# Two of the four block sums of the feed-forward made in one piece, and a small key copy moved to GpSimd

## The chip, the cores and the metric

The kernel runs on one core of a Trainium2 chip. The metric is the device time of one execution in microseconds (us); lower is better. The core has five engines that run their own instruction queues side by side and wait for each other through semaphores: TensorE (PE in the profile, its weight loads PEld), VectorE (DVE), ScalarE (ACT), GpSimd (POOL) and SyncE (SP, which here issues most of the DMAs).

## What is computed

Attention with a few global key columns and a local window, and behind it a mixing layer with a low-rank part and a feed-forward part. Batch 4, 8 heads, 768 positions, head size 64, 8 global columns, a window of 96; model width 512, hidden width 2048, rank 32.

```python
scores = scale * np.matmul(q, k.transpose(0, 1, 3, 2))
is_global = pos[None, :] < int(n_global)
is_local = (rel >= 0) & (rel < int(n_local))
scores = scores - slopes[:, None, None] * dist      # by head
scores = np.where(is_global | is_local, scores, -1000000000.0)
a = np.exp(scores - max); a = a / (sum(a) + 1e-09)
x = np.matmul(a, v)                                 # (4, 768, 512)
u = x + (x.transpose(0, 2, 1) @ U @ V).transpose(0, 2, 1)
out = u + np.maximum(u @ w_ch1, 0.0) @ w_ch2
```

## The kernel before

**Attention.** Two heads of one batch make a pair, 128 partitions wide when transposed; there are 16 pairs, `i` from 0 to 15, four to a batch. For each pair q and k are loaded, cast to 16 bits and turned to `qT` and `kT` (head dimension on the partitions): by TensorE for pairs 0 to 7 (`st_T`), by transposing DMAs for pairs 8 to 15 (`turn`). Positions lie in six blocks of 128. A query block needs its own key block (`kT`) and the one before it, and the eight global columns. For the second kind there is a tile `kA`: the key blocks 0 to 4 with the first eight columns of each written over by the global columns. For pairs 8 on, `st_K` makes it with two instructions: ScalarE copies columns 8 to 127 of each block (L339), VectorE the eight global columns into all five blocks, 128x40 elements (L340).

The scores (L365 with `kT`, L372 with `kA`) come in three parts into the PSUM tile `sc`; VectorE adds the bias and writes `sp` (L403), ScalarE takes the exponential (`ep`, L415), TensorE multiplies by v (`ob`, L428 and L432), VectorE divides (L437, L451) into `x_sb`. GpSimd casts that to 16 bits (`x16`, L454) and casts the next v (L142).

**The low-rank part.** Per pair: `st_M1` multiplies `x16` by U (L463), ScalarE copies the small result (L467), `st_MT` transposes it on TensorE (L480) and VectorE copies it to `tmp16` (L481, `tmp` in the profile); `st_M3` multiplies by V into the PSUM tile `sc` (L517, with `tmp` as its moving operand), VectorE adds it to `x_sb` (L522), GpSimd casts the sum (L525), and a DMA transposes it to `uT` (`st_X`).

**The feed-forward part.** Positions are taken in groups of 256, three to a batch. An "up" unit is eight matmuls of 256 columns (L631) and a relu by ScalarE (L636) into `htr`; a group has eight ups. The groups of batch 0 are multiplied by the second weight directly (L666). For the nine groups of batches 1 to 3, called `WG`, the second product is done in seven block products instead of eight. `htr` is split into four blocks of 128 positions by 1024 hidden units: a11, a12 (first 128 positions), a21, a22 (last 128). Four sums of them are made on VectorE (L555):

- s1 = a21 + a22
- s2 = s1 - a11
- s3 = a11 - a21, written over a21
- s4 = a12 - s2

and four such sums `t1` to `t4` of the weight's blocks once. The products, each eight matmuls of 256 columns (L684), run in the order x1 (a11), y1 (a12), x2 (s2), y2 (s1), x3 (s3), y3 (s4), x4 (a22); the x accumulate in the bank `cx`, the y in `cy`, and after each VectorE adds the part to `x_sb` (L689). When a result is whole a DMA stores it.

**The order.** Everything is issued in one order written out by hand, so each engine's queue is what the loop over `i` issues. Between the steps of the attention, `fill` issues a given number of units: an up of a coming group or a product of the one before, mostly in turn. The relu's values come in two halves: the ups are issued so that after the fourth of a group the first half of the hidden units of each of a11, a12, a21 and a22 is there and after the eighth the rest (`mk_up`, `queue_sums(0)` and `queue_sums(1)`). Each half queues its four sums of 512 elements, in the order s1, s2, s4, s3, in the deque `jobs`, due two units later; after each unit one job that is due is issued (two if more than four are waiting). A product that needs sums issues what is still queued first, through `need`. The tiles s1, s2 and s4 have one buffer each. In the loop `st_MT` (L480, L481) and `st_M3` (L517) have one unit between them; `st_K` follows `st_MT` at once.

Of the kernel before, what the change touches and what calls it, by code (L numbers as in the profile page):

```python
# [16 lines left out]
ALU = mybir.AluOpType  # L17
# [3 lines left out]
def kernel(  # L21
# [13 lines left out]
    nc = tc.nc  # L35
# [30 lines left out]
    HJ = NJC // 2  # L66
# [20 lines left out]
    def ps_cps(name):  # L87
        return psum.tile([P, 512], FP32, name=name, tag="cps", bufs=2)
# [247 lines left out]
    def st_K(i):  # L336
        kT = kts[i]
        kA = kp.tile([P, NSB - 1, P], FP16, name="kA", tag="kA")
        nc.scalar.copy(kA[:, :, NG:], kT.rearrange("d (n p) -> d n p", n=NSB)[:, 0:NSB - 1, NG:])  # L339
        nc.vector.tensor_copy(  # L340
            kA[:, :, 0:NG], kT[:, 0:NG].unsqueeze(1).broadcast_to((P, NSB - 1, NG))
        )
        kas[i] = kA
# [208 lines left out]
    def queue_sum(name, part, out_, a, b_, op, wait=0):  # L552

        def go():
            nc.vector.tensor_tensor(out_, a, b_, op)  # L555
            have.add((name, part))
        (slow if name[0] == "t" else jobs).append((count[0] + wait, go))

    def need(*names):

        for queue, kind in ((jobs, tuple), (slow, str)):
            while not all(n in have for n in names if isinstance(n[0], kind)):
                queue.popleft()[1]()
# [19 lines left out]
    def weight(w, j):  # L583
        return tw[w][:, j] if w != "t3" else tw[w][j // 2][:, j % 2]
# [11 lines left out]
    def queue_group(b, g):  # L596
# [3 lines left out]
        cell = {}  # L600
# [3 lines left out]
        last = (b, g) == (B - 1, NFG - 1)  # L604

        def queue_sums(k):

            h = cell["htr"]
            if k == 0:
                for x in (1, 2, 4):  # L610
                    cell[f"s{x}"] = ffp.tile([P, HJ, P], FP16, name=f"s{x}", tag=f"s{x}", bufs=1)
                cell.update(a11=h[:, 0:HJ, 0:P], a12=h[:, HJ:NJC, 0:P],
                            a21=h[:, 0:HJ, P:FT], s3=h[:, 0:HJ, P:FT], a22=h[:, HJ:NJC, P:FT])
            js = slice(k * HJ // 2, (k + 1) * HJ // 2)
            for name, a, b_, op in (
                ("s1", "a21", "a22", ALU.add), ("s2", "s1", "a11", ALU.subtract),
                ("s4", "a12", "s2", ALU.subtract), ("s3", "a11", "a21", ALU.subtract),
            ):
                queue_sum((name, b, g), k, cell[name][:, js], cell[a][:, js], cell[b_][:, js], op, wait=0 if last else 2)

        def mk_up(at):
            jp = at // 2 + (at % 2) * NJC // 4 if split else at

            def go():
                if jp == 0:
                    cell["htr"] = ffp.tile([P, NJC, FT], FP16, name="htr", tag="htr", bufs=3)
                hps, done = begun.pop(jp) if jp in begun else (ps_th("hps"), 0)
                for k in range(2):
                    jt = 2 * jp + k
                    for dc in range(done, NDC):  # L630
                        nc.tensor.matmul(  # L631
                            hps[:, k * FT:(k + 1) * FT],
                            w1_16[:, dc, jt * P:(jt + 1) * P], uT[:, dc, ts],
                            start=(dc == 0 and k == 0), stop=(dc == NDC - 1 and k == 1),
                        )
                nc.scalar.activation(  # L636
                    cell["htr"][:, 2 * jp:2 * jp + 2].rearrange("p j t -> p (j t)"), hps, AF.Relu
                )
                if split and at % 4 == 3:
                    queue_sums(at // 4)  # L640
            return go

        def store(n, cs=slice(0, DM)):
            def go():
                nc.sync.dma_start(out[b, n * P:(n + 1) * P, cs], x_sb[:, n, cs])
            if b:
                go()
            else:
                kept.append(go)
# [25 lines left out]
        def mk_product(bank, half, a, w, dst, first=False, done=None):  # L675

            def go():
                if bank not in cell:
                    cell[bank] = ps_cps(bank)
                need(*(((a, b, g), k) for k in range(2) if a[0] == "s"))  # L680
                need(*((w, k) for k in range(4 if w == "t3" else 2) if w[0] == "t"))
                ps = cell[bank][:, half]
                for j in range(HJ):
                    nc.tensor.matmul(  # L684
                        ps, cell[a][:, j], weight(w, j), start=(first and j == 0),
                        stop=(done is not None and j == HJ - 1), skip_group_check=True,
                    )
                n, cs = dst
                nc.vector.tensor_tensor(x_sb[:, n, cs], ps, x_sb[:, n, cs], ALU.add)  # L689
                for what in done or ():  # L690
                    store(*what)
            return go
# [111 lines left out]
    for i in range(NP, NPAIR + 2):  # L804
        b, hp = divmod(i, NP)
# [73 lines left out]
        if NPE <= i + 1 < NPAIR:  # L879
            st_K(i + 1)  # L880
# [52 lines left out]
```

## Time and profile before

| What | Value |
| --- | --- |
| Runs shown: median (lowest to highest), 3 runs | 231.4 us (230.68 to 231.84) |
| The profiled execution's own time | 231.74 us |
| Its span, first to last instruction | 230.0 us |
| Granted TensorE clock, mean over the span | 1.00 |
| Relu, L636, ScalarE | 96 instructions, 56.4 us busy |
| Sums of the relu's values, L555, VectorE | 72 instructions of 512 elements, 33.4 us busy |
| Global key columns, L340, VectorE | 8 instructions, 1.3 us busy |
| `tmp`, L481, VectorE | 12 instructions, 3.4 us busy |

A line of a timeline has the start and the duration in microseconds, the engine, the line of the kernel, the operation, what it writes and reads, the shape and the count of merged instructions; in brackets how long its engine stood idle before it and what ended that. VectorE's instructions overlap a little at their ends. A line of a source view has the smallest, the median and the largest duration in ns and the first and last start. Busy shares are means over the whole span: the attention runs up to about 175 us, the direct products to about 90 us, the seven-product groups from about 99 us to the end.

### The profile page before, as it was taken

What the parts mean: (1) busy time and instruction counts of PE and PEld (TensorE: products, weight loads), DVE (VectorE), ACT (ScalarE), POOL (GpSimd) and SP (SyncE); (2) the same over time, 40 slices, a digit from 0 to 9 for tenths busy, and PEclk for the clock granted to TensorE, in tenths of its full rate; (3) what the DMA queues carried; (4) which work ended last, traced back from release to release, by engine and by line L of the source; (5) the groups of instructions that cost most, each with busy time, mean ns of one, the idle gap of its engine ahead of it and who ended that gap; (6) DMA issues with size and microseconds to landing.
All of it is one profiled execution on the core that took longest, in us unless ns stands there. A gap on an engine that the chain in (4) does not pass through costs nothing.

```text
span 230.0 us, 5877 instructions
## 1 busy us (share of the span) xinstructions
PE 220.7 (96%) x2418; PEld 171.1 (74%) x2420; DVE 161.5 (70%) x337; ACT 125.8 (55%) x196; POOL 72.3 (31%) x115
## 2 busy tenths in 40 slices
PE   7989899999999999999999999999999999999993
PEld 2456568788745445888888878888988888888882
DVE  3799876749577979597989897989764444444452
ACT  6787747786805253968485847292732433333320
POOL 6499708297553323123313131313111000000000
PEclk9999999999999999999999999999999999999999
DMA  6999996979999879897979994951321202010022
GB/s 185 335 283 281 281 291 90 321 135 180 191 163 206 201 180 228 203 239 175 261 202 219 242 200 102 144 158 25 88 69 36 94 0 94 0 67 27 10 84 93
DMA packets 86563, 36.68 MB, mean 160 GB/s; under 512 B 74152, under 2 KB 83592, under 8 KB 86536
## 3 DMA queue, kind: packets, MB, share of 16 engines
q1 hardware_dynamic: 81480, 32.01, 57.5%
q0 software_dynamic: 5056, 4.29, 12.4%
q8 instruction: 19, 0.31, 0.6%
q14 instruction: 8, 0.07, 0.1%
HBM read 27.46 MB, written 6.29 MB: 147 GB/s over the span
## 4 chain that ended last, share of the span: by engine, by line
PE 67%; DVE 15%; DMA 7%; ACT 4%; POOL 2%; issue 1%; SPq 0%; ACTq 0%
PE hps L631 25%; PE cx L684 13%; PE cy L684 10%; PE cps L666 8%; DMA w<-in_moe_w_ch_dram 6%; DVE sp L403 3%; PE sc L365 2%; ACT ep L415 2%; DVE x_sb L451 2%; PE tp L254 2%; PE ob L432 2%; DMA kst<-in_k_dram 2%; PE sc L517 1%; PE ob L428 1%; DVE s L555 1%
## 5 line engine op out<-in xcount | busy, mean ns | idle before, releaser
L631 PE MATMUL hps<-uT,w 128*128 128x256 f16 x756 | 96.0, 273 | 0.0
L636 ACT ACTIVATE htr<-hps 128x512 f16<-128x512 f32 x96 | 56.4, 598 | 58.0 <-PE hps L631 57.9
L631 PEld LDWEIGHTS <-w 128*128 128x128 f16 x756 | 70.5, 98 | 9.9 <-issue 0.2
L403 DVE SCALAR_TENSOR_TENSOR sp<-sc,relcat 128x1024 f32<-128x1024 f32 (+1 forms) x36 | 40.7, 1131 | 9.1 <-ACT ep L415 4.8
L415 ACT ACTIVATE ep<-sp 128x1408 f16<-128x1408 f32 x24 | 33.1, 1380 | 0.7 <-DVE sp L403 0.6
L684 PEld LDWEIGHTS <-htr 128*128 128x128 f16 x288 | 27.5, 98 | 3.6
L454 POOL CAST x<-x_sb 128x384 f16<-128x384 f32 x27 | 14.5, 538 | 49.8 <-DVE x_sb L451 45.7
L689 DVE TENSOR_TENSOR x_sb<-cx,x_sb 128x256 f32<-128x256 f32 x36 | 15.2, 422 | 18.3 <-PE cx L684 17.7
L666 PE MATMUL cps<-w,htr 128*128 128x512 f16 x96 | 24.0, 379 | 0.4 <-DMA w<-in_moe_w_ch_dram 0.4
L525 POOL CAST x<-x_sb 128x768 f16<-128x768 f32 x12 | 11.0, 916 | 40.8 <-DVE x_sb L522 40.8
L684 PEld LDWEIGHTS <-s 128*128 128x128 f16 x216 | 20.2, 98 | 2.9 <-DVE s L555 0.6
L689 DVE TENSOR_TENSOR x_sb<-cy,x_sb 128x256 f32<-128x256 f32 x27 | 11.4, 423 | 12.5 <-PE cy L684 12.3
L365 PEld LDWEIGHTS <-kT 64*128 64x128 f16 x192 | 8.3, 93 | 13.7 <-issue 12.4
L451 DVE TENSOR_TENSOR x_sb<-ob,rcp 128x384 f32<-128x384 f32 x30 | 16.7, 558 | 1.0
L365 PE MATMUL sc<-qT,kT 64*128 64x128 f16 x192 | 16.8, 221 | 0.3 <-DVE x_sb L522 0.2
L432 PE MATMUL ob<-v,ep 128*128 128x65 f16 x192 | 16.4, 193 | 0.0
L432 PEld LDWEIGHTS <-ep 128*128 128x128 f16 x192 | 13.8, 98 | 3.1 <-ACT x L787 0.7
L428 PE MATMUL ob<-vA,ep 128*128 128x65 f16 x160 | 14.5, 194 | 1.2 <-DVE vA L316 1.2
L142 POOL CAST v<-vst 128x768 f16<-128x768 f32 x16 | 14.0, 877 | 2.9 <-DMA vst<-in_v_dram 2.9
L372 PE MATMUL sc<-qT,kA 64*128 64x128 f16 x160 | 14.3, 217 | 0.6 <-DVE kA L290 0.4
L666 PEld LDWEIGHTS <-htr 128*128 128x128 f16 x96 | 8.4, 97 | 8.5 <-issue 0.5
L522 DVE TENSOR_TENSOR x_sb<-sc,x_sb 128x768 f32<-128x768 f32 x12 | 11.5, 956 | 4.6 <-PE sc L517 4.6
(109 smaller groups left out, 315.0 us busy)
## 6 DMA issues: line engine op xcount, KB each, us to landing
qst<-in_q_dram SPq DMA_DIRECT2D x16, 384.0 KB, 4.7
kst<-in_k_dram SPq DMA_DIRECT2D x16, 384.0 KB, 6.1
vst<-in_v_dram SPq DMA_DIRECT2D x16, 384.0 KB, 4.0
out_dram<-x_sb SPq DMA_DIRECT2D x23, 256.0 KB, 3.1
w<-in_moe_w_ch_dram POOLq DMA_DIRECT2D x8, 512.0 KB, 8.1
vA<-v SPq DMA_DIRECT2D x8, 152.3 KB, 3.0
out_dram<-x_sb SPq DMA_DIRECT2D x2, 128.0 KB
uT<-x SPq DMA_TRANSPOSE x12, 3.1
```

Of the source, the lines that this page charges most:

```text
L365: nc.tensor.matmul(scs[hi][:, o:o + P], kT[r, kb * P:(kb + 1) * P], qT[r, kb * P:(kb + 1) * P], start=(o == 0 and not on_pe), stop=(o + P ...
L403: nc.vector.scalar_tensor_tensor(out=sps[i][:, :, c0:c0 + tot], in0=both[:, :, 0:tot], scalar=qk_scale / slope[2 * (i % NP)], in1=relfs[c0 ...
L415: nc.scalar.activation(eps[i][:, hi], sps[i][:, hi], AF.Exp, scale=slope[2 * (i % NP)])
L428: nc.tensor.matmul(ob[:, qi], ep[:, OF[qi - 1]:OF[qi - 1] + P], vA[:, qi - 1, hi], start=True, stop=False,)
L432: nc.tensor.matmul(ob[:, qi], ep[:, DG[qi]:DG[qi] + P], vt[:, qi, hi], start=(qi == 0), stop=True,)
L451: nc.vector.tensor_tensor(xo, ob[:, :, 0:D], rb, ALU.mult)
L454: nc.gpsimd.tensor_copy(x16, xo)
L631: nc.tensor.matmul(hps[:, k * FT:(k + 1) * FT], w1_16[:, dc, jt * P:(jt + 1) * P], uT[:, dc, ts], start=(dc == 0 and k == 0), stop=(dc == ...
L636: nc.scalar.activation(cell["htr"][:, 2 * jp:2 * jp + 2].rearrange("p j t -> p (j t)"), hps, AF.Relu)
L666: nc.tensor.matmul(cps, htr[:, jc, t * P:(t + 1) * P], w2_16[:, jc], start=(b > 0 and jc == 0), stop=(jc == NJC - 1),)
L684: nc.tensor.matmul(ps, cell[a][:, j], weight(w, j), start=(first and j == 0), stop=(done is not None and j == HJ - 1), skip_group_check=True,)
L689: nc.vector.tensor_tensor(x_sb[:, n, cs], ps, x_sb[:, n, cs], ALU.add)
```

## The change

Two edits. The global key columns of pairs 8 to 15 are copied by GpSimd instead of VectorE. And for all groups of `WG` but the last, s3 and s4 are no longer made by halves: nothing is queued for them at the first half, and at the second one instruction of 1024 elements each, in the order s1, s2, s3, s4 (s1 and s2 by halves as before). The last group keeps its halves, with s3 ahead of s4. The products wait for one part of s3 and s4 instead of two.

```diff
@@ st_K @@
-        nc.vector.tensor_copy(
+        nc.gpsimd.tensor_copy(
             kA[:, :, 0:NG], kT[:, 0:NG].unsqueeze(1).broadcast_to((P, NSB - 1, NG))
         )
@@ queue_sums @@
-            js = slice(k * HJ // 2, (k + 1) * HJ // 2)
             for name, a, b_, op in (
                 ("s1", "a21", "a22", ALU.add), ("s2", "s1", "a11", ALU.subtract),
-                ("s4", "a12", "s2", ALU.subtract), ("s3", "a11", "a21", ALU.subtract),
+                ("s3", "a11", "a21", ALU.subtract), ("s4", "a12", "s2", ALU.subtract),
             ):
-                queue_sum((name, b, g), k, cell[name][:, js], cell[a][:, js], cell[b_][:, js], op, wait=0 if last else 2)
+                parts = {k: slice(k * HJ // 2, (k + 1) * HJ // 2)}
+                if name in ("s3", "s4") and not last:
+                    parts = {0: slice(0, HJ)} if k else {}
+                for part, js in parts.items():
+                    queue_sum(
+                        (name, b, g), part, cell[name][:, js], cell[a][:, js], cell[b_][:, js],
+                        op, wait=0 if last else 2,
+                    )
@@ mk_product @@
-                need(*(((a, b, g), k) for k in range(2) if a[0] == "s"))
+                need(*(((a, b, g), k) for k in range(2 if last or a in ("s1", "s2") else 1)
+                       if a[0] == "s"))
```

In VectorE's queue this takes out 24 instructions. Where before the second halves of a group stood as s1, s2, s4, s3 with the other work between them, they now stand as s1, s2, s3 (whole), s4 (whole); in three of the five groups whose sums lie within the attention, `L481` comes straight behind s4, as it came straight behind the second half of s3 before.

## The prediction

> **What bounds the kernel now.** I read the page's busy shares first, then TensorE's timeline for the places where it stands still, and last VectorE's and GpSimd's timelines around those places.
>
> ```profile
> PE 220.7 (96%) x2418; PEld 171.1 (74%) x2420; DVE 161.5 (70%) x337; ACT 125.8 (55%) x196; POOL 72.3 (31%) x115
> ...
> 104.56 1.04 PE L631 MATMUL hps<-uT,w 128*128 128x256 f16 x8
> 105.81 0.50 PE L517 MATMUL sc<-tmp,v16w 128*128 128x128 f16 x6 [0.21 <-DVE tmp L481]
> ...
> 136.57 0.61 PE L684 MATMUL cx<-t,s 128*128 128x256 f16 x4
> 137.46 0.61 PE L684 MATMUL cx<-t,s 128*128 128x256 f16 x4 [0.28 <-DVE s L555]
> ...
> 138.99 1.04 PE L684 MATMUL cy<-t,s 128*128 128x256 f16 x8
> 139.86 0.50 PE L517 MATMUL sc<-tmp,v16w 128*128 128x128 f16 x6
> ...
> 171.33 1.04 PE L631 MATMUL hps<-uT,w 128*128 128x256 f16 x8
> 172.48 0.49 PE L517 MATMUL sc<-tmp,v16w 128*128 128x128 f16 x6
> ```
>
> Columns: start, duration, engine, line, operation, count. TensorE bounds. Eight 256-column matmuls follow each other at 0.87 us a group (138.99 to 139.86), 0.109 each, so where TensorE stands still can be computed. After 104.56 the next was due at 105.43 and began at 105.81: 0.38 us lost, site A. Four from 136.57 were due to end their turn at 137.01, the fifth began at 137.46: 0.45 lost, site B0. At 139.86 (site B) L517 starts on time. After 171.33 it was due at 172.20 and came at 172.48: 0.28 lost, site C. I found no other wait of over 0.15 us for VectorE after 95 us; the remaining irregularities are fixed steps of about 0.1 us around the half-height score matmuls. So all that VectorE costs TensorE while the sums run is 0.38 + 0.45 + 0.28 = 1.11 us. After C TensorE waits for nothing up to the end, so a microsecond lost at any site is a microsecond at the end.
>
> VectorE just before A, B and C:
>
> ```profile
> 104.48 0.42 DVE L555 TENSOR_TENSOR s<-htr,s 128x512 f16<-128x512 f16 x1
> 104.81 0.42 DVE L689 TENSOR_TENSOR x_sb<-cx,x_sb 128x256 f32<-128x256 f32 x1
> 105.14 0.42 DVE L555 TENSOR_TENSOR htr<-htr 128x512 f16<-128x512 f16 x1
> 105.48 0.28 DVE L481 CAST tmp<-ob 128x128 f16<-128x128 f32 x1
> ...
> 138.20 0.41 DVE L689 TENSOR_TENSOR x_sb<-cx,x_sb 128x256 f32<-128x256 f32 x1
> 138.53 0.41 DVE L555 TENSOR_TENSOR s<-htr,s 128x512 f16<-128x512 f16 x1
> 138.86 0.41 DVE L555 TENSOR_TENSOR htr<-htr 128x512 f16<-128x512 f16 x1
> 139.20 0.28 DVE L481 CAST tmp<-ob 128x128 f16<-128x128 f32 x1
> ...
> 171.47 0.42 DVE L689 TENSOR_TENSOR x_sb<-cx,x_sb 128x256 f32<-128x256 f32 x1 [0.68 <-PE cx L684]
> 171.81 0.42 DVE L555 TENSOR_TENSOR htr<-htr 128x512 f16<-128x512 f16 x1
> 172.14 0.28 DVE L481 CAST tmp<-ob 128x128 f16<-128x128 f32 x1
> ```
>
> L481 makes `tmp`, which L517 loads; only one unit of the feed-forward (0.87 us) lies between TensorE's L480, which L481 waits for, and L517. What stands just ahead of L481 on VectorE is therefore critical, and at A, B and C that is a sum of this change. L517 starts 0.05 us after L481 ends (105.76 to 105.81). At B L481 ends at 139.48 and L517 is due at 139.86, so B has 0.38 - 0.05 = 0.33 us to spare. At C VectorE had stood idle 0.68 us for TensorE's `cx` and could not have begun sooner.
>
> **The change, part by part.** *Sums.* Eight of the nine groups have s3 and s4 made as one 1024-element instruction each instead of two of 512. The source view has the durations:
>
> ```profile
> L555 DVE TENSOR_TENSOR s<-htr x18: 415/416/935, 96.0 to 220.8; 128x512 f16<-128x512 f16 x18
> ...
> L555 DVE TENSOR_TENSOR t<-w,t x4: 682/682/1121, 72.6 to 89.1; 128x1024 f16<-128x1024 f16 x4
> ```
>
> (minimum, median, maximum in ns.) A half takes 0.416 us, and its successor starts 0.335 us after it (105.14 to 105.48, 0.08 overlapped). A whole is not there for these tiles; the weight sums of the same size take 0.682, so 0.60 from start to start. Per group 4 x 0.335 - 2 x 0.60 = 0.14 us of VectorE is saved, 1.1 us over eight. That alone is worth nothing: VectorE is not the bound. What counts is where the longer instructions fall. In the order of the changed kernel the second halves of s1 and s2 are followed by L403 (where a score tile is due), s3 whole, the `cx` addition, s4 whole, L481; before, one half stood on either side of `cx`, or two behind it.
>
> At C `cx` is released by TensorE, so all ahead of it is hidden in the 0.68 us of idling; behind it a whole replaces a half: L481 is later by 0.682 - 0.416 = 0.27 us, and L517 with it. At B `cx` follows L403 and is released before both sums; two wholes replace two halves, 0.53 us later, less 0.33 to spare: 0.20 us. At A the bounds are wider. `cx` (a group of eight begun at 103.64, its last result at 104.68) can be added at 104.72 at best; then s4 runs 105.05 to 105.73 and L481 starts at 105.65 instead of 105.48: +0.17. At worst L403 still starts at 103.61: s3 from 104.48, `cx` from 105.08, s4 from 105.41, L481 at 106.01: +0.53. The first halves of s3 and s4 (99.48 to 100.46) are gone from ahead of this, but the second half of s1 waits for ScalarE's relu (101.83 + 0.60 = 102.43) and starts at 102.45 instead of 102.61, so 0.16 of the gain survives: 0.53 - 0.16 = 0.37, and I take 0.35.
>
> The other pairs have no whole sum between L480 and L481 and start L517 on time with some 0.3 us to spare, as at B. The users of s3 and s4 are far off: at A s3 would be done by 105.16 at worst for the product at 108.32, s4 by 106.1 for the one at 110.83. In the late groups the second half of s2 starts at 196.94, so s3 would run from 197.3 to 198.0 and, behind the `cx` addition of 198.41, s4 from 198.75 to 199.4, for products that TensorE's timeline has at 200.76 and 202.51. The relu's buffer is held no longer than by these same products.
>
> *Key columns.* Eight copies of 128x40 (166 ns each) leave VectorE: at most 1.3 us, behind L481 and ahead of L522, which waits for TensorE's L517 anyway. On GpSimd the nearest row is its own 128x32 copy of the same kind (L295, 212 ns). They stand there behind the cast of v (L142) and ahead of the cast of x (L525), before which GpSimd idles 3.0 to 4.8 us in this stage; 0.21 us vanishes in that. If this cover went, x's transposing DMA would start 0.21 later each time. The copy comes sooner than before: behind the cast ending at 104.39 instead of at 105.68, for score matmuls (L372) at 108.06. Its only new wait there is for the DMA that lands kT (3.3 to 4.5 us after issue, 99.96 + 3.5 = 103.5). No DMA is added or moved on SP or GpSimd. L372 now waits for ScalarE and GpSimd, eight more wait instructions on TensorE's queue; queue waits of other engines show 17 to 21 ns. Bounds 0 and 8 x 0.021 = 0.17 us; the weight loads run ahead, so I take 0.
>
> *GpSimd against VectorE.*
>
> ```profile
> 95.87 0.83 POOL L525 CAST x<-x_sb 128x768 f16<-128x768 f32 x1 [3.99 <-DVE x_sb L522]
> 96.04 0.94 DVE L555 TENSOR_TENSOR s<-htr 128x512 f16<-128x512 f16 x1 [0.23 <-ACT htr L636]
> ```
>
> A sum that starts while GpSimd copies takes 0.94 instead of 0.42 us and ends 0.28 after the copy. B0 is that too: the second half of s2 took 0.94 from 136.47, against the cast of v (136.11 to 137.14). A new copy of 0.21 us can lengthen a sum by that. At B0 it would run from 137.14 and push s2, which TensorE waits for, by 0.21 if it is taken first; the sum was already waiting, so I take 0 and keep 0.21 for the range. The Trainium skill speaks against this part of the change: "SBUF — State Buffer", section "Who interferes with whom", has the port that VectorE's second SBUF input comes through shared with GpSimd, and whoever starts first keeps it for the whole instruction. The two rows above agree; what would follow here is the second rival.
>
> **Sum.** 0.35 (A) + 0.20 (B) + 0.27 (C) + 0 = 0.82 us. On the profiled execution, 231.74 us with a span of 230.0 and 1.74 around it, that is 232.56; it lies 0.34 above the median of the runs, 231.4, which so becomes **232.2 us**, 0.35% slower. Ends: 0.17 + 0 + 0.27 = 0.44 and 0.53 + 0.20 + 0.27 + 0.17 = 1.17: 231.8 to 232.6.
>
> **Rivals.** *VectorE's relief pays.* If the sums, thinned by 2.4 us, reached A, B0 and C in time, all 1.11 us would go: 230.3. For it: VectorE is 9.15 of 10 us busy from 130 to 140. Against: C's addition waited for TensorE, A's sums for ScalarE, B0's for GpSimd. 0.10.
>
> *GpSimd holds VectorE off at the wrong moment.* A at its worst, because GpSimd's cast of v moves ahead with the additions that it follows and meets the second half of s1 (+0.53), the new copy getting in first at B0 (+0.21), B 0.20, C 0.27: 1.21, so 232.6, and with one more sum held for a whole cast of v (0.5) ahead of L481 233.1. For it: eleven sums after 95 us are already lengthened. Against: most of these meet no wait of TensorE. It decides once a hold ends less than one sum ahead of L481. 0.25.
>
> *B0 goes.* With sums moved, the second half of s2 may miss the cast of v: -0.45 against +0.82, 231.8. Against: what precedes it there (additions, L451) is unchanged and still sets the cast off. 0.13.
>
> **Chances.** The forecast has 0.52. About 0.5% of the time, 1.16 us, is what a measurement tells from none. Faster than 230.24: half of the first rival and a little for the scatter of runs (230.68 to 231.84), 0.07. Slower than 232.56: two thirds of the second rival, 0.17, and the upper part of the forecast with that scatter, 0.20: 0.37. Within: 0.56. The range, 231.1 to 233.1, leaves out the first rival and the tails.
>
> **What would show it.** In the changed profile: six L555 instructions a group with two near 0.68 us; L517 late by 0.6 to 0.9 at A, some 0.2 at B, 0.55 at C; GpSimd's key copy near 0.21 us and done over 2 us before L372; L684 never waiting for s3 or s4. Wrong it would be if L517 came sooner than before at A or C, if L372 waited for GpSimd, or if TensorE lost time where these traces show none.

## The result and the profile after

| | Kernel before | Changed kernel |
| --- | --- | --- |
| Median of all runs | 231.39 us (22 runs) | 232.43 us (22 runs) |
| Ratio to before, 95% interval | | 1.0048 (1.0027 to 1.007) |
| Profiled execution: time, span | 231.74, 230.0 us | 232.32, 230.5 us |

The changed kernel is slower by about half a percent, 0.6 to 1.6 us by the interval. Ratios are over runs in the fast state; the trace of e2 below is of a run in the slow one (235.18 us), with a granted clock of 0.91 between 20 and 40 us and of 1.00 from 80 us on, where the places read lie.

TensorE's timeline after the change, at the same places as before (the ups are now line L637, the products L691, the additions L696):

```profile
104.31 1.04 PE L637 MATMUL hps<-uT,w 128*128 128x256 f16 x8
105.86 0.49 PE L517 MATMUL sc<-tmp,v16w 128*128 128x128 f16 x6 [0.51 <-DVE tmp L481]
...
136.61 0.61 PE L691 MATMUL cx<-t,s 128*128 128x256 f16 x4
137.50 0.61 PE L691 MATMUL cx<-t,s 128*128 128x256 f16 x4 [0.28 <-DVE s L555]
...
139.03 1.04 PE L691 MATMUL cy<-t,s 128*128 128x256 f16 x8
140.12 0.49 PE L517 MATMUL sc<-tmp,v16w 128*128 128x128 f16 x6
...
171.58 1.04 PE L637 MATMUL hps<-uT,w 128*128 128x256 f16 x8
173.00 0.50 PE L517 MATMUL sc<-tmp,v16w 128*128 128x128 f16 x6 [0.39 <-DVE tmp L481]
```

With 0.109 us a matmul, L517 was due at 105.18, 139.91 and 172.45. It came 0.68 late at A (0.38 before), 0.21 at B (0 before) and 0.55 at C (0.28 before). B0 lost 0.45, as before. At B no bracket stands, because the matmul before it ends, as modelled, at 140.07; only the start tells. The three growths are 0.30 + 0.21 + 0.27 = 0.78 us.

VectorE's timeline there:

```profile
103.99 0.68 DVE L555 TENSOR_TENSOR htr<-htr 128x1024 f16<-128x1024 f16 x1
104.59 0.41 DVE L696 TENSOR_TENSOR x_sb<-cx,x_sb 128x256 f32<-128x256 f32 x1
104.92 0.68 DVE L555 TENSOR_TENSOR s<-htr,s 128x1024 f16<-128x1024 f16 x1
105.52 0.28 DVE L481 CAST tmp<-ob 128x128 f16<-128x128 f32 x1
...
138.57 0.68 DVE L555 TENSOR_TENSOR htr<-htr 128x1024 f16<-128x1024 f16 x1
139.16 0.70 DVE L555 TENSOR_TENSOR s<-htr,s 128x1024 f16<-128x1024 f16 x1
139.78 0.28 DVE L481 CAST tmp<-ob 128x128 f16<-128x128 f32 x1
...
170.50 0.69 DVE L555 TENSOR_TENSOR htr<-htr 128x1024 f16<-128x1024 f16 x1
171.72 0.42 DVE L696 TENSOR_TENSOR x_sb<-cx,x_sb 128x256 f32<-128x256 f32 x1 [0.54 <-PE cx L691]
172.07 0.68 DVE L555 TENSOR_TENSOR s<-htr,s 128x1024 f16<-128x1024 f16 x1
172.66 0.28 DVE L481 CAST tmp<-ob 128x128 f16<-128x128 f32 x1
```

At C whole s3 lies in the time in which VectorE waited for `cx` anyway (idle 0.68 us there before, 0.54 now); whole s4 lies behind `cx` and ahead of L481. At B both lie ahead of L481 without idle time. The page has VectorE at 155.9 us busy instead of 161.5: less work, more time.

### The profile page after: what moved, and what is told of

Its sections match the earlier page's. It is cut to its first block, busy times and chain, and to the rows that moved or that the text cites. A ratio compares the mean times of both kernels' runs of the same rounds, so it can differ in the third digit from the quotient of the medians.

```text
span 230.5 us, 5876 instructions
## 1 busy us (share of the span) xinstructions
PE 220.7 (96%) x2418; PEld 170.9 (74%) x2420; DVE 155.9 (68%) x313; ACT 125.7 (55%) x196; POOL 72.9 (32%) x123
## 4 chain that ended last, share of the span: by engine, by line
PE 70%; DVE 11%; DMA 9%; POOL 3%; ACT 3%; issue 1%; SPq 1%
PE hps L637 27%; PE cx L691 13%; PE cy L691 10%; PE cps L672 8%; DMA w<-in_moe_w_ch_dram 6%; DMA vst<-in_v_dram 3%; PE sc L365 3%; DVE sp L403 3%; PE ob L432 2%; DVE s L555 2%; PE sc L517 2%; DVE x_sb L451 1%; PE ob L428 1%; PE tp L254 1%; PE sc L372 1%
## 5 line engine op out<-in xcount | busy, mean ns | idle before, releaser
L637 PE MATMUL hps<-uT,w 128*128 128x256 f16 x756 | 95.9, 273 | 0.0
L637 PEld LDWEIGHTS <-w 128*128 128x128 f16 x756 | 70.6, 98 | 9.7
L403 DVE SCALAR_TENSOR_TENSOR sp<-sc,relcat 128x1024 f32<-128x1024 f32 (+1 forms) x36 | 40.7, 1131 | 8.9 <-ACT ep L415 4.8
L691 PEld LDWEIGHTS <-htr 128*128 128x128 f16 x288 | 27.5, 98 | 3.6
L696 DVE TENSOR_TENSOR x_sb<-cx,x_sb 128x256 f32<-128x256 f32 x36 | 15.2, 422 | 21.4 <-PE cx L691 21.2
L691 PEld LDWEIGHTS <-s 128*128 128x128 f16 x216 | 20.2, 98 | 2.9 <-DVE s L555 0.6
L696 DVE TENSOR_TENSOR x_sb<-cy,x_sb 128x256 f32<-128x256 f32 x27 | 11.4, 423 | 11.9 <-PE cy L691 11.6
L365 PEld LDWEIGHTS <-kT 64*128 64x128 f16 x192 | 8.3, 93 | 13.7 <-issue 12.4
L365 PE MATMUL sc<-qT,kT 64*128 64x128 f16 x192 | 16.8, 221 | 0.3 <-DVE x_sb L522 0.2
L372 PE MATMUL sc<-qT,kA 64*128 64x128 f16 x160 | 14.2, 217 | 0.3
```

What stands on the lines that cost most here:

```text
L365: nc.tensor.matmul(scs[hi][:, o:o + P], kT[r, kb * P:(kb + 1) * P], qT[r, kb * P:(kb + 1) * P], start=(o == 0 and not on_pe), stop=(o + P ...
L372: nc.tensor.matmul(scs[hi][:, o + P:o + 2 * P], kA[r, kb], qT[r, (kb + 1) * P:(kb + 2) * P], start=False, stop=(o + 2 * P == tot),)
L403: nc.vector.scalar_tensor_tensor(out=sps[i][:, :, c0:c0 + tot], in0=both[:, :, 0:tot], scalar=qk_scale / slope[2 * (i % NP)], in1=relfs[c0 ...
L637: nc.tensor.matmul(hps[:, k * FT:(k + 1) * FT], w1_16[:, dc, jt * P:(jt + 1) * P], uT[:, dc, ts], start=(dc == 0 and k == 0), stop=(dc == ...
L691: nc.tensor.matmul(ps, cell[a][:, j], weight(w, j), start=(first and j == 0), stop=(done is not None and j == HJ - 1), skip_group_check=True,)
```

## The experiments

All times lost are read as above, from TensorE's starts. "Elsewhere" is what TensorE lost after 75 us away from the four places, score matmuls aside. Ratios are to the kernel before, run beside each other.

| Kernel | A | B0 | B | C | elsewhere | ratio (95% interval) |
| --- | --- | --- | --- | --- | --- | --- |
| before | 0.38 | 0.45 | 0 | 0.28 | 0.20 | |
| changed | 0.68 | 0.45 | 0.21 | 0.55 | 0 | 1.0048 (1.0027 to 1.007) |
| e1, sums only | 0.68 | 0.45 | 0.20 | 0.55 | 0.23 | 1.0021 (0.9988 to 1.0053) |
| e2, keys only | 0.38 | 0.45 | 0 | 0.28 | 0 | 0.9997 (0.9964 to 1.003) |
| e3, sums later | 0 | 0.33 | 0 | 0 | 0.68 | 0.9977 (0.995 to 1.0005) |
| e4, fills ahead of L481 | 0.71 | 0.45 | 0 | 0.63 | 0 | 1.0026 (0.9992 to 1.0059) |
| e5, sums later, v earlier | 0 | 0 | 0 | 0 | 0.07 | 0.9959 (0.9935 to 0.9984) |
| e6, s3 whole | 0.75 | 0.45 | 0 | 0.28 | 0 | one run |
| e7, s4 whole | 0.74 | 0.44 | 0 | 0.55 | 0.12 | one run |
| e8, v earlier | 0.36 | 0 | 0 | 0.28 | 0 | 0.9971 (0.9944 to 0.9998) |

Theory S: the longer sums ahead of L481 make `tmp` late at A, B and C. Theory K: the key copies on GpSimd cost the time, through contention or the added waits.

**e1, the sums alone.** The changed kernel with the key copies back on VectorE.

```diff
-        nc.gpsimd.tensor_copy(
+        nc.vector.tensor_copy(
             kA[:, :, 0:NG], kT[:, 0:NG].unsqueeze(1).broadcast_to((P, NSB - 1, NG))
         )
```

> Only the sums of the change; the key copies stay on VectorE. Theory S (the whole sums make tmp, L481, late at three places): the whole loss is here. TensorE loses about 0.68 us at A (near 105.8 us), 0.45 at B0 (137.5), 0.21 at B (140.1), 0.55 at C (173.0), so the time is about 0.8 us above the kernel before (ratio near 1.0035 to 1.005). Theory K (the key copies on GpSimd cost it, by the port or by eight more waits on TensorE): about the kernel before, ratio 1.000 +- 0.001, with 0.38, 0.45, 0 and 0.28 at the four places.

The four places lose what they lose in the changed kernel to within 0.02 us. The interval of the time holds both the forecast and no change, so the verdict rests on the places, and they speak for S.

**e2, the key copies alone.** The kernel before with the opposite edit.

> Only the key copies moved to GpSimd; the sums as before. Theory S: nothing changes, ratio 1.000 +- 0.001, losses 0.38, 0.45, 0, 0.28 us at A, B0, B and C. Theory K: the loss is here, ratio near 1.004, with TensorE late at L372 or sums lengthened by a copy of 0.2 us ahead of a wait of TensorE.

A, B0, B and C are as before to 0.01 us, and the ratio is 0.9997. By time K falls only as far as a third of a percent (0.8 us) can be told, but the places leave nothing for it.

**e3, the same sums, later.** The changed kernel with s3 and s4 due later; no instruction is shorter.

```diff
-                        op, wait=0 if last else 2,
+                        op, wait=0 if last else 6 if name in ("s3", "s4") else 2,
```

> The changed kernel with s3 and s4 due six units after the last relu instead of two, so that L481 stands ahead of s4 at A and B and ahead of both at C or behind none of them. Nothing is smaller and VectorE does the same work. Theory S: the losses at A, B and C go (0.68 + 0.21 + 0.55 = 1.44 us against the changed kernel), perhaps 0.1 comes back where a product then waits for s3; against the kernel before 0.38 + 0.28 - 0.1 = about 0.55 us faster, ratio near 0.9975. Theory K or a cause elsewhere: as slow as the changed kernel, ratio near 1.004.

VectorE's and then TensorE's timeline at A:

```profile
103.64 0.42 DVE L696 TENSOR_TENSOR x_sb<-cx,x_sb 128x256 f32<-128x256 f32 x1 [0.38 <-PE cx L691]
103.98 0.28 DVE L481 CAST tmp<-ob 128x128 f16<-128x128 f32 x1
104.18 0.68 DVE L555 TENSOR_TENSOR htr<-htr 128x1024 f16<-128x1024 f16 x1
```

```profile
103.49 1.04 PE L637 MATMUL hps<-uT,w 128*128 128x256 f16 x8
104.37 0.50 PE L517 MATMUL sc<-tmp,v16w 128*128 128x128 f16 x6
```

The whole sum still takes 0.68 us, behind L481 now, and L517 starts on time (103.49 + 0.87 = 104.36). All three places are clean. The ratio, 0.9977, is the forecast one. Its interval holds 1, so that e3 is faster than the kernel before is not shown by time; it lies wholly below the interval of the changed kernel, which K had forecast for e3 as well. Part of the 1.44 us came back in places not foreseen: 0.38 us for a relu at 134.3 and 0.23 for a DMA of v's rows at 119.2, with 0.07 for s3 as expected. By the table's rows e3 is therefore ahead of the kernel before by 0.30 us (1.31 less 1.01) and not by the 0.55 forecast; that the ratio still came out as forecast is luck.

**e4, a delay of its own.** The kernel before with two fills on VectorE ahead of every L481.

```diff
+        for _ in range(2):
+            nc.vector.memset(zw[:, 2 * P:4 * P], 0.0)
         nc.vector.tensor_copy(tmps[b][:, dc * P:(dc + 1) * P], tps[:, 0:P])
```

> The kernel before with two idle fills of 128x256 16-bit elements on VectorE just ahead of every L481; what they write is used by nothing. They take some 0.13 to 0.2 us each from start to start, 0.25 to 0.4 together. Theory S, that lateness of L481 goes to the end one for one beyond what a place has to spare: A and C lose the whole of it more, 0.25 to 0.4 each, the other places, with about 0.33 us to spare, 0 to 0.07 each: in all 0.5 to 1.0 us above the kernel before, ratio 1.002 to 1.004. If the time lost at L517 is taken back later: ratio 1.000.

```profile
105.23 0.41 DVE L557 TENSOR_TENSOR htr<-htr 128x512 f16<-128x512 f16 x1
105.61 0.42 DVE L482 MEMSET zw<- 128x128 uint32 x2
105.95 0.23 DVE L483 CAST tmp<-ob 128x128 f16<-128x128 f32 x1
```

L481 (here L483) starts 0.72 us after s3 instead of 0.34 and takes 0.23 us instead of 0.28, so it ends 0.33 later. A loses 0.33 more and C 0.34 more; B, with 0.33 us to spare, and the other places after 95 us lose nothing. At L517 lateness of `tmp` is passed on one for one beyond the slack, whatever causes it. The ratio, 1.0026, fits, but its interval holds 1.

**e6 and e7, one sum each.** The changed kernel with only s3, or only s4, whole.

```diff
-                if name in ("s3", "s4") and not last:
+                if name in ("s3",) and not last:
```

In e7 the name is `"s4"`; in both the products wait for the parts that there are.

> Of the change only s3 whole; s4 by halves, the key copies on GpSimd. Theory S, place by place: at C s3 stands ahead of the cx addition, in VectorE's idle time, and a half of s4 behind it as before: 0.28 us lost at L517, as before the change. At B one whole and one half: 0.27 later with 0.33 to spare, nothing lost. At A both stand in a chain without idle time: 0.4 to 0.7. B0 0.45. If it is the number or the order of the sums and not their length, B and C are as in the changed kernel (0.21, 0.55).

> Of the change only s4 whole; s3 by halves, the key copies on GpSimd. Theory S: at C the whole stands behind the cx addition: 0.55 us lost, as in the changed kernel. At B one whole and one half: nothing lost. At A 0.5 to 0.8. B0 0.45. If order or number decide: B 0.21.

L517 at C, in e6 and then in e7:

```profile
173.17 0.49 PE L517 MATMUL sc<-tmp,v16w 128*128 128x128 f16 x6
```

```profile
172.88 0.49 PE L517 MATMUL sc<-tmp,v16w 128*128 128x128 f16 x6 [0.39 <-DVE tmp L481]
```

Only whole s4 costs at C, and B costs nothing with either alone: the length of what lies behind the last external wait decides, not the count of sums. A, at 0.75, was above the range given for e6. VectorE's and GpSimd's timeline of e6 has the reason:

```profile
103.09 1.02 DVE L555 TENSOR_TENSOR s<-s,htr 128x512 f16<-128x512 f16 x1
```

```profile
103.01 0.83 POOL L142 CAST v<-vst 128x768 f16<-128x768 f32 x1
```

The second half of s2 took 1.02 us instead of 0.42, because GpSimd's cast of v held it off up to 103.84; the chain from there to L481 has no idle time to take that up. In e7 it took 1.02 us too (from 102.54, against a cast from 102.46 to 103.29), so A does not tell s3 from s4.

**e8 and e5, GpSimd's cast moved.** B0 is the same collision in the kernel before, as VectorE's and GpSimd's timelines of that kernel show:

```profile
136.47 0.94 DVE L555 TENSOR_TENSOR s<-s,htr 128x512 f16<-128x512 f16 x1
```

```profile
136.11 1.03 POOL L142 CAST v<-vst 128x768 f16<-128x768 f32 x1
```

In e8 the kernel before casts v two units earlier, in e5 the kernel of e3 does.

```diff
+        if live and i >= NPE:
+            cast_v(i)
+            st_A(i)
         if i + 1 < NPE:
             st_T(i + 1)
...
-        if live:
+        if live and i < NPE:
             cast_v(i)
             st_A(i)
```

> The kernel before with the cast of v two units earlier, as in e5; sums and key copies as before. If GpSimd's cast is the cause of B0: B0 goes (0.45 us to under 0.1), A and C stay at 0.38 and 0.28, and the kernel is about 0.4 us faster than before, ratio near 0.998. If not: ratio 1.000, B0 0.45.

> The kernel of e3_sums_later with GpSimd's cast of v (and the copies of v's rows that follow it) issued two units earlier for pairs 8 on, so that it no longer falls on the second half of s2. If the 0.45 us at B0 (0.33 in e3) is GpSimd's cast holding the sum off: it goes, and with A, B and C gone too the kernel is 0.7 to 1.0 us faster than the one before, ratio 0.9955 to 0.997, and faster than e3. If B0 is VectorE's own queue: B0 stays at 0.3 to 0.45 and the ratio is e3's, 0.9977.

GpSimd's and then VectorE's timeline of e5 around B0:

```profile
133.36 0.84 POOL L142 CAST v<-vst 128x768 f16<-128x768 f32 x1
135.51 0.51 POOL L454 CAST x<-x_sb 128x384 f16<-128x384 f32 x1 [1.30 <-DVE x_sb L451]
```

```profile
135.72 0.57 DVE L555 TENSOR_TENSOR s<-htr 128x512 f16<-128x512 f16 x1
136.32 0.42 DVE L555 TENSOR_TENSOR s<-s,htr 128x512 f16<-128x512 f16 x1
```

The cast is over at 134.20, the second half of s2 takes its plain 0.42 us, and B0 is gone in both kernels; the first half still meets the cast of x and is lengthened to 0.57, which no product waits for. e5 is faster than the kernel before: 230.67 us median, ratio 0.9959 (0.9935 to 0.9984), an interval that also lies below that of the changed kernel. It overlaps with those of e3 and e8, so that e5 is faster than e3, as expected, is not shown, nor which of its two parts brings more. e8 was expected near 0.998 and came to 0.9971: besides B0's 0.45 us its profile lacks the 0.20 that the kernel before lost elsewhere, a wait for a DMA that comes and goes (see below).

## Why the prediction was right

*What bounds, and where.* Right. L517's wait for `tmp` at A and C and the slack at B were the places; no product came to wait for s3 or s4 in the changed kernel, and nothing else after 95 us changed between the two.

*The sizes.* C was put at 0.27 and measured 0.27, B at 0.20 and measured 0.21. The whole sums take 0.68 us as the weight sums did, and the order was the one read. A was put at 0.35 between 0.17 and 0.53 and measured 0.30, but there two errors of the prediction nearly cancel, and that is luck. GpSimd's and VectorE's timelines of the changed kernel have both:

```profile
102.10 0.83 POOL L142 CAST v<-vst 128x768 f16<-128x768 f32 x1
```

```profile
101.37 0.41 DVE L555 TENSOR_TENSOR s<-htr 128x512 f16<-128x512 f16 x1
...
102.51 0.69 DVE L555 TENSOR_TENSOR s<-s,htr 128x512 f16<-128x512 f16 x1
```

First, the second half of s1 did not wait for the relu that the prediction named. In the changed kernel that relu runs from 101.30 to 101.90, and the sum started at 101.37. The next addition, of `cy`, started at 102.17 instead of 102.94. TensorE's own work lay 0.25 earlier there (L517 due at 105.18, not 105.43), so VectorE's lead was 0.52 us, not 0.16. Second, the second half of s2 then met the cast of v and took 0.69 us instead of 0.42. That cost 0.27 of the lead: L403 started at 103.12 instead of 103.61, 0.24 earlier when TensorE's 0.25 is taken off, and 0.53 - 0.24 = 0.29. Without the hold the growth at A would have been some 0.16 instead of 0.30, by an estimate from these rows: `cx` was whole at 104.41 (103.38 + 1.03) and could have been added at 104.45, as 0.04 us lie between the two at C, instead of at 104.59. The hold comes with the sums and not with the key copy, for e1 has it as well (0.69 us from 103.27). The sum of the terms, 0.82, measured 0.78.

*Against the time.* The medians differ by 1.04 us and the ratio says 1.1, with 0.6 to 1.6 as its interval, so 0.78 is inside. The two profiled executions differ by only 0.58 us. Of that, TensorE's last matmul came 0.52 later: 0.78, less 0.20 that the kernel before lost at 90.49 waiting for the DMA of `uT`, less 0.06 by which the changed kernel stood ahead at 65.8. That wait is in the profiles of the kernel before and of e1, with 0.12 us in that of e7, and not in those of e4 and e8, which have the key copies on VectorE as the kernel before does; it comes and goes with the landing of that DMA, not with the change. Whether the remaining 0.3 us between 0.78 and the ratio is real or scatter was not tried.

*The key copies.* Costed at nothing, and e2 shows nothing at any of the places. GpSimd's copy took 0.216 us in the median as drawn from its 212 ns row:

```profile
L340 POOL COPY kA<-kT x8: 212/216/571, 70.1 to 149.0; 128x40 f16<-128x40 f16 x8
```

The largest, 0.571, is the copy of 138.75, beside whole s3 at B (138.57 to 139.25); that was not foreseen, and it lay in GpSimd's idle time. The eight added waits on TensorE take 51 ns each, not 17 to 21, and cost nothing all the same: summed over the forty places behind 72 us where a matmul of L372 follows one of L365, start to start is 2.351 us before and 2.356 us after.

*The rivals.* Relief for VectorE paid nothing, because at C TensorE's `cx` and at B0 GpSimd's cast set the time, and at A the longer sums and the hold used up the lead. What the relief is worth once the sums stand elsewhere is not shown: e3 changes their place, and the old halves issued as late were not run. The second rival's collision did happen at A, with s2 and not s1, and made about half of the growth there (0.14 of 0.30 us, by the estimate above). In e6 it cost more: A lost 0.75 us, where the changed kernel's 0.68 less 0.27 for the shorter s4 would have been 0.41. B0 did not go, for the reason given: the cast follows the same addition in both kernels. The Trainium skill, "SBUF — State Buffer", section "Who interferes with whom", has a VectorE instruction with two SBUF inputs contend with a GpSimd instruction that reads SBUF. e5 and e8 agree: with the cast moved off, the same sum fell from 0.94 to 0.42 us.

## What to carry to other kernels

Fewer and longer instructions save an engine's time on the whole and still cost the kernel, if the engine is not the bound and a long one lands between a short handover's two ends. Look for the handover with the least room (one unit of TensorE's work here), list what its engine does behind the last wait that comes from outside, and count only that. Then move the long work behind the handover, as e3 did here, and keep GpSimd's large casts away from the sums that TensorE waits for.

## What the runs showed of the hardware

TensorE's wait for the second weight's DMA at about 66 us takes up what comes before it: the changed kernel reached its first product there 0.93 us ahead of the kernel before (60.65 against 61.58 us) and went on 0.06 ahead (65.77 against 65.83). Over the profiles that wait was from 0.13 us (e8) to 1.87 us (e6).

GpSimd is held off too: its cast of v took 0.84 us alone and 1.05 beside a sum, its copy of 128x40 elements 0.21 alone and up to 0.57, so the collision between VectorE's sums and GpSimd's copies goes both ways.
